# Clustered attention before two expert layers: products with the centroids at once in four column tiles, beside a block of products with v

## The chip, the cores and the metric

One core of a Trainium2 chip runs the kernel in one launch. The metric is device time in microseconds (us), over three runs of the kernel before: median 624.69, from 623.21 to 628.34. In the profile the engines are PE (TensorE matmuls), PEld (its weight loads), DVE (VectorE), ACT (ScalarE), POOL (GpSimd) and SP (the queue from which nearly all DMAs are issued).

## The reference

Attention in which a token only sees the tokens of its own cluster, then two layers of routed experts. Two batches, 8 heads, 768 tokens, head size 64, 16 centroids per head, all in 32-bit floats:

```python
q_n, k_n, c_n = (x / (norm(x) + 1e-6) for x in (q, k, centroids))
q_assign = argmax(einsum('bhsd,hcd->bhsc', q_n, c_n))
k_assign = argmax(einsum('bhsd,hcd->bhsc', k_n, c_n))
mask = q_assign[:, :, :, None] == k_assign[:, :, None, :]
scores = where(mask, q @ k.T / sqrt(64), -1e9)
attn = softmax(scores)
x = attn @ v                      # then (1536, 512)
x = moe(x, w_gate, w1, w2, capacity)      # top 1 of 8 experts, 512 -> 1024 -> 512, at most `capacity` tokens each
x = moe2(x, w_gate, w_output_gate, w1, w2)  # top 1 of 8, no capacity
```

## The kernel before

The attention is worked off in 8 **pairs**: a pair is one batch and two neighbouring heads j = 0, 1. A pair has 12 **slots**: one for each block c of 128 queries (c = 0 to 5) and each head j. One pass of the main loop (`for i in range(len(seq) + LAG + 1)`) is a slot. The program is not rescheduled: each engine works through its instructions in the order in which the Python code issues them. In a slot stand, in this order:

- `scores` (pss, L238): four matmuls into one of two PSUM tiles; its tile is free when the exp of the slot two before has read it. Then `softmax_max` (nm, L246) on DVE.
- `tr_p` (ppt, L268): the transposes of the exp of two slots before, in two halves of three, each half into one of the three PSUM tiles of the pool `ps_t`; each half is copied out to pt (L270), the first by ACT, the second by DVE, but by ACT too where c is 2 or 5.
- in slots 0, 4, 6 and 10 `av` (L280), a block of products with v; in slots 1 and 7 `fin`, with px (L307) on PE and its evictions on DVE.
- the loads of a later pair (slots 7, 8, 9: q, k, v), and the **preparation of the next pair**, one entry of the list `prep` per slot.
- `softmax_exp` (pe, L254) on ACT, behind what the preparation gave to ACT.

The preparation splits q and k into a rounded part and a rest (qh and kh on ACT, ql on DVE, kl on POOL), copies them by DMA into the operands of the scores (12 DMAs, `operands`), and finds each token's cluster: `logits` (plog, L153: products of the 32 padded centroids of two heads with q and with k, 384 tokens at a time), evicted to lt with a scale (L156 on ACT for the first half of the tokens, L160 on DVE for the second), `logits_t` (plt, L167: six transposes), `argmax` and `first` (DVE and POOL), and `oh_t` (poh, L194: six transposes of the one-hot rows, evicted by DVE to ot, L195), from where four DMAs bring the one-hot rows into the operands x2 and y2. The scores of the next pair wait for those.

All these transposes, plog and px take their PSUM tiles from the same three of `ps_t`; the one that was read longest ago is taken next. The DMAs of SP use eight completion semaphores in turn, and a DMA waits until the one eight before it on SP has landed. In pair 6 SP also issues the first four loads of expert weights (raw, 1 MB each, L808 and L810). In its slot 9 the pools of the preparation are closed, and the first converted weights (wh, L837, on ACT) take over their memory, so wh waits for the DMAs that read ot.

The slots of the preparation before: 0 qh; 1 ql, kh, kl; 2 logits; 3 logits_t; 4 argmax and operands; 5 first; 8 oh_t. In pair 0 it starts two slots later. The next pair is prepared in pairs 0 to 6. The first pair is prepared ahead of the loop.

Of the kernel before, what the change touches and what calls it, by code (L numbers as in the profile page):

```python
# [8 lines left out]
F32 = mybir.dt.float32  # L9
F32R = mybir.dt.float32r  # L10
I32 = mybir.dt.int32
AF = mybir.ActivationFunctionType
ALU = mybir.AluOpType
AX = mybir.AxisListType
PSUM = bass.MemoryType.PSUM
BIG = float(2.0 ** 100)
WARM = 8
P0 = 2
# [10 lines left out]
def attention(tc, end, ps_t, ident, wu, q, k, v, centroids, wg, x_half, lg_sb, consts, before_half, after_half, extra, slot):  # L29


    nc = tc.nc
    B, NP, P, _, C, D = v.shape
    H = 2 * NP
    S = P * C
    G = centroids.shape[1] // H
    E = wg.shape[1]
    HALF = C // 2
# [4 lines left out]
    with ExitStack() as ctx:  # L43
# [11 lines left out]
        def cpy(dst, src):  # L55
            nc.sync.dma_start(dst.bitcast(F32), src.bitcast(F32))

        def centroid_norms():

            nc.vector.tensor_tensor(c_sq, cw, cw, op=ALU.mult)  # L60
            p = ps_t.tile([P, 512], F32, tag="t", name="pc")[:64, :NP]
            for hp in range(NP):
                for t in range(2):
                    nc.tensor.matmul(p[32 * t:32 * t + 2 * G, hp:hp + 1], c_sq[:, hp].rearrange("p j g -> p (j g)"),
                                     ones, start=True, stop=True)
            nc.scalar.sqrt(c_n, p)
            nc.vector.tensor_scalar_add(c_n, c_n, 1e-6)
            nc.vector.reciprocal(c_n, c_n)
# [23 lines left out]
        c_sq = one.tile([P, NP, 2, G], F32, name="c_sq")  # L92
        c_n = one.tile([64, NP], F32, name="c_n")
        ones = one.tile([P, 1], F32, name="a_ones")
        rev = one.tile([P, G], F32, name="rev")
        msc = one.tile([64, 2], F32, name="msc")
        rw = end.tile([P, NP, P + 2 * E], F32, name="rw")
# [47 lines left out]

        def logits(pi):
            b, hp = pairs[pi]
            d = st[pi]
            d["lt"] = lt = w1.tile([64, S], F32, tag="lt", name="lt")
            for hf in range(2):  # L150
                p = ps_t.tile([P, 512], F32, tag="t", name="plog")[:64, :W]
                for t, nm in enumerate("qk"):
                    nc.tensor.matmul(p[32 * t:32 * t + 2 * G], cw[:, hp].rearrange("p j g -> p (j g)"),  # L153
                                     d[nm][:, hf * W:(hf + 1) * W], start=True, stop=True)
                if hf == 0:
                    nc.scalar.mul(lt[:, :W], p, c_n[:, hp:hp + 1])  # L156
                elif pi == 0:
                    nc.scalar.mul(lt[:, W:], p, c_n[:, hp:hp + 1])
                else:
                    nc.vector.tensor_scalar_mul(lt[:, W:], p, c_n[:, hp:hp + 1])  # L160

        def logits_t(pi):
            d = st[pi]
            p = ps_t.tile([P, 512], F32, tag="t", name="plt")[:, :C * 4 * G]
            d["lg"] = p.rearrange("p (c t j g) -> p c t j g", c=C, t=2, j=2)
            for c in range(C):
                nc.tensor.transpose(p[:, c * 4 * G:(c + 1) * 4 * G], d["lt"][:, c * P:(c + 1) * P], ident[:64, :64])  # L167

# [18 lines left out]
        def oh_t(pi):  # L187
            d = st[pi]
            ot = w1.tile([64, S], F32R, tag="lt", name="ot")
            ohv = d["oh"].rearrange("p (c i) g -> p c (i g)", i=4)  # L190
            for hf in range(2):
                p = ps_t.tile([P, 512], F32, tag="t", name="poh")[:64, :W]
                for c in range(HALF):
                    nc.tensor.transpose(p[:, c * P:(c + 1) * P], ohv[:, hf * HALF + c], ident)  # L194
                nc.vector.tensor_scalar(ot[:, hf * W:(hf + 1) * W], p, msc[:, 0:1], msc[:, 1:2],  # L195
                                        op0=ALU.mult, op1=ALU.add)
            s = pi % 2
            for j in range(2):
                cpy(xs["x2", s, j][64:64 + G], ot[j * G:(j + 1) * G])
                cpy(xs["y2", s, j][64:64 + G], ot[(2 + j) * G:(3 + j) * G])  # L200

# [17 lines left out]
        def first_rows(j):  # L219
            for hf in range(2):  # L220
                p = ps_t.tile([P, 512], F32, tag="t", name="poh")[:64, :W]
                for c in range(HALF):
                    nc.tensor.transpose(p[:, c * P:(c + 1) * P],
                                        oh0[j][:, hf * HALF + c].rearrange("p t g -> p (t g)"), ident)
                hs = slice(hf * W, (hf + 1) * W)
# [120 lines left out]
        def last():  # L346
# [3 lines left out]
        prep = [  # L350
            lambda i: part(i, "qh"),
            lambda i: (part(i, "ql"), part(i, "kh"), part(i, "kl")),
            lambda i: logits(i),
            lambda i: logits_t(i),
            lambda i: (argmax(i), operands(i, 0), operands(i, 1)),
            lambda i: first(i),
            lambda i: None,
# [19 lines left out]
        for j in range(2):  # L377
            nc.gpsimd.memset(oh0[j], 0.0)
        for (p0, c0, x) in ((0, 0, 1.0), (0, 1, 0.0), (32, 0, BIG), (32, 1, -BIG)):
            nc.vector.memset(msc[p0:p0 + 32, c0:c0 + 1], x)  # L380
        keep_warm(WARM)
# [48 lines left out]
        for i in range(len(seq) + LAG + 1):  # L430
# [15 lines left out]
            if cur:  # L446
# [7 lines left out]
                if i == 1:  # L454
                    first_rows(1)
                ps = sl - P0 + (sl - P0 > 6) if pi == 0 else sl
                if pi + 1 < NPR and 0 <= ps < len(prep):
# [1470 lines left out]
```

## Time and profile before

| | us |
|---|---|
| median of three runs | 624.69 |
| the profiled execution, its own time | 626.9 |
| its span | 625.1 |
| PE busy | 568.9 (91%) |
| DVE busy | 467.7 (75%) |
| ACT busy | 420.6 (67%) |
| POOL busy | 214.3 (34%) |
| start of slot 0 of pairs 1 to 7 | 41.50, 72.20, 103.23, 135.00, 168.60, 200.52, 234.33 |

The attention lasts until about 276 us; behind it the two expert layers follow, with 349 us. A time in a timeline is counted from the start of the span. A busy time of PE counts overlapping matmuls once; a product of 32-bit floats appears as two instructions, so the products of one half of the tokens (q and k) are four rows.

### The profile page before, as it was taken

Reading aid. Unit: us, or ns where it says so; the run is one execution under the profiler, and the core shown is the slowest. Engines: PE = TensorE matmul, PEld = TensorE weight load, DVE = VectorE, ACT = ScalarE, POOL = GpSimd, SP = SyncE. Lnnn points to the kernel's source line nnn. Section 1 sums busy time; section 2 is a strip of 40 time slices with the busy share of each in tenths; the row PEclk is TensorE's granted clock in tenths of the full one; section 3 lists DMA queues with packets and bytes.
Section 4 is the critical chain, followed back from the end, with each engine's and each line's share of the span. In section 5 each row is a group of like instructions: output and inputs, shape, how many; then the busy total and the mean of one; then the engine's idle time right before and its main releaser. Section 6 shows DMA issues by size and latency. Waiting matters only on the chain.

```text
span 625.1 us, 14529 instructions
## 1 busy us (share of the span) xinstructions
PE 568.9 (91%) x5430; PEld 469.5 (75%) x5430; DVE 467.7 (75%) x1214; ACT 420.6 (67%) x891; POOL 214.3 (34%) x425
## 2 busy tenths in 40 slices
PE   6899999998999988976999998998887899999993
PEld 2666767675766666655878997997766888999992
DVE  5867777679989677866597689788876566889881
ACT  4766666776666669843676776876853466979781
POOL 8702020204150210135725257444333523253441
PEclk9899999999999999999899999999989799999997
DMA  5879381926429961323386776977844457998930
GB/s 144 214 227 274 102 212 48 212 62 151 141 84 229 248 183 70 134 105 108 116 268 209 241 251 174 301 246 236 280 158 165 147 178 238 302 304 297 328 116 20
DMA packets 75518, 117.55 MB, mean 188 GB/s; under 512 B 10504, under 2 KB 43400, under 8 KB 75441
## 3 DMA queue, kind: packets, MB, share of 16 engines
q1 hardware_dynamic: 72017, 106.76, 56.6%
q0 software_dynamic: 3264, 9.72, 4.9%
q8 instruction: 45, 0.74, 0.5%
q14 instruction: 32, 0.26, 0.1%
q10 hardware_dynamic: 160, 0.07, 0.0%
HBM read 84.28 MB, written 12.87 MB: 155 GB/s over the span
## 4 chain that ended last, share of the span: by engine, by line
PE 61%; DVE 16%; ACT 10%; DMA 5%; issue 4%; POOL 2%; SPq 0%; ACTq 0%; POOLq 0%; DVEq 0%
PE ph L947 16%; PE py L1019 11%; PE av L280 9%; PE pss L238 7%; PE ppt L268 6%; DVE nm L246 3%; DVE wl L844 3%; PE pz L994 3%; ACT pe L254 2%; PE pyo L1635 2%; PE pxt L924 2%; ACT wh L837 2%; ACT pt L270 1%; DMA xg<-x2d,idx 1%; DMA out<-xo,tk 1%
## 5 line engine op out<-in xcount | busy, mean ns | idle before, releaser
L844 DVE SCALAR_TENSOR_TENSOR wl<-raw,sw,wh 128x1024 f16<-128x1024 f32 x128 | 163.5, 1283 | 17.9 <-ACT wh L837 17.1
L837 ACT ACTIVATE wh<-raw,sw 128x1024 f16<-128x1024 f32 x128 | 145.8, 1146 | 3.1 <-DMA x<-ot 2.5
L246 DVE TENSOR_REDUCE nm<-pss 128x1 f32<-128x768 f32 x96 | 91.4, 952 | 41.1 <-PE pss L238 37.4
L947 PEld LDWEIGHTS <-wh 128*128 128x128 f16 x1152 | 90.4, 101 | 18.2 <-issue 13.4
L254 ACT ACTIVATE pe<-pss,nm 128x768 f32<-128x768 f32 x96 | 87.1, 907 | 24.2 <-DVE nm L246 24.2
L238 PE MATMUL pss<-y,x 128*128 128x384 f32 x384 | 93.6, 365 | 4.7 <-ACT pe L254 3.2
L268 PE MATMUL ppt<-ident,pe 128*128 128x128 f32 x576 | 80.3, 275 | 3.3 <-ACT pe L254 1.3
L238 PEld LDWEIGHTS pss<-y,x 128*128 128x128 f32 x384 | 63.2, 190 | 25.1 <-issue 13.0
L947 PE MATMUL ph<-xh,wh 128*128 128x192 f16 (+14 forms) x576 | 69.1, 244 | 9.8 <-DVE hl L956 6.7
L270 ACT COPY pt<-ppt 128x384 f32<-128x384 f32 x128 | 57.9, 482 | 29.2 <-PE ppt L268 28.8
L1019 PEld LDWEIGHTS <-wh 128*128 128x128 f16 x960 | 72.4, 99 | 4.6 <-issue 1.3
L268 PEld LDWEIGHTS ppt<-ident,pe 128*128 128x128 f32 x576 | 69.2, 142 | 8.9 <-ACT pt L270 2.3
L947 PE MATMUL ph<-xl,wh 128*128 128x192 f16 (+14 forms) x576 | 68.9, 244 | 0.2
L947 PE MATMUL ph<-xh,wl 128*128 128x192 f16 (+14 forms) x576 | 68.9, 244 | 0.0
L280 PE MATMUL av<-pt,v 128*64 128x384 f32 x384 | 68.8, 494 | 0.0
L949 ACT ACTIVATE hh<-ph 128x128 f16<-128x128 f32 (+14 forms) x144 | 44.0, 312 | 34.3 <-PE ph L947 31.5
L956 DVE SCALAR_TENSOR_TENSOR hl<-ph,hh 128x192 f16<-128x192 f32 (+14 forms) x138 | 44.4, 334 | 26.7 <-ACT hh L949 26.1
L1019 PE MATMUL py<-hh,wh 128*128 128x192 f16 (+13 forms) x480 | 46.7, 239 | 1.9 <-ACT hh L949 1.1
L947 PEld LDWEIGHTS <-wl 128*128 128x128 f16 x576 | 46.7, 101 | 2.1
L1019 PE MATMUL py<-hl,wh 128*128 128x192 f16 (+13 forms) x480 | 46.6, 239 | 0.8 <-DVE hl L956 0.6
L1019 PE MATMUL py<-hh,wl 128*128 128x192 f16 (+13 forms) x480 | 46.1, 239 | 0.0
L280 PEld LDWEIGHTS av<-pt,v 128*64 128x64 f32 x384 | 24.8, 136 | 28.4 <-issue 28.2
(322 smaller groups left out, 864.1 us busy)
## 6 DMA issues: line engine op xcount, KB each, us to landing
raw<-in_moe_w SPq DMA_DIRECT2D x64, 1024.0 KB
y<-kh SPq DMA_DIRECT2D x31, 192.0 KB
x<-qh SPq DMA_DIRECT2D x30, 192.0 KB
q<-in_q SPq DMA_DIRECT2D x8, 384.0 KB
k<-in_k SPq DMA_DIRECT2D x8, 384.0 KB
x<-ql SPq DMA_DIRECT2D x16, 192.0 KB
v<-in_v SPq DMA_DIRECT2D x8, 384.0 KB
out<-zt SPq DMA_DIRECT2D x1, 3072.0 KB
```

The lines of the kernel that those rows point to most:

```text
L238: nc.tensor.matmul(p[:, hf, :W], xx[:, c * P:(c + 1) * P], yy[:, hf * W:(hf + 1) * W], start=a, stop=o)
L246: nc.vector.tensor_reduce(nm, p[:, :, :W], axis=AX.XY, op=ALU.max, negate=True)
L254: nc.scalar.activation(pe, p[:, :, :W], AF.Exp, bias=d["nm", c, j], scale=1.0, accum_out=d["sm"][:, c, j:j + 1])
L268: nc.tensor.transpose(p[:, kc * P:(kc + 1) * P], pe[:, kh, kc * P:(kc + 1) * P], ident)
L270: eng(pt[:, kh * HALF:(kh + 1) * HALF, (c % HALF) * P:(c % HALF + 1) * P], p.rearrange("p (a b) -> p a b", a=HALF))
L280: nc.tensor.matmul(p[j * D:(j + 1) * D, :W], d["v"][:, j, kc, :], d["pt", hf, j][:, kc, :], start=(kc == 0), stop=(kc == C - 1))
L837: nc.scalar.activation(hi[:, :, s], x[:, :, s], AF.Copy, scale=sw)
L844: nc.vector.scalar_tensor_tensor(lo[:, :, s], x[:, :, s], sw, hi[:, :, s], op0=ALU.mult, op1=ALU.subtract, accum_out=fl)
L947: nc.tensor.matmul(p[:, :N], w[:, c, fs], x[:, c, :N], start=(k == 0), stop=(k == 11))
L949: nc.scalar.activation(hh[:, f, :N], p[:, :N], AF.Relu)
L956: nc.vector.scalar_tensor_tensor(hl[:, f, :N], p[:, :N], 0.0, hh[:, f, :N], op0=ALU.max, op1=ALU.subtract)
L1019: nc.tensor.matmul(p[:, :N], w[:, f, s], x[:, f, :N], start=(k == 0), stop=(k == 23))
```

## The change

- `logits` writes the products of both halves of the tokens into one PSUM tile: q and k of the first half into partitions 0 and 32, of the second into 64 and 96. One eviction over 128 partitions follows, on DVE (on ACT ahead of the loop), where there were two over 64 partitions, on ACT and DVE.
- `logits_t` and `oh_t` transpose 128 by 128 blocks, three each instead of six, and ot is evicted by one DVE instruction instead of two. The chunks of tokens stand in another order, which the indices follow.
- ot then holds each row in two halves, so eight DMAs of 16 x 384 bring it into x2 and y2, where there were four of 16 x 768.
- The preparation stands in other slots: 0 logits, behind the block of av; 1 logits_t and qh; 2 argmax, kh, kl; 3 ql; 4 first and operands; 7 oh_t. The list has eight entries instead of nine, so the pools of the preparation close in slot 8 of pair 6.
- In the start, the norms of the centroids are made for 128 partitions, and eight constants are set by POOL where DVE set four.

```diff
         def logits(pi):
-            d["lt"] = lt = w1.tile([64, S], F32, tag="lt", name="lt")
+            d["lt"] = lt = w1.tile([P, W], F32, tag="lt", name="lt")
+            p = ps_t.tile([P, 512], F32, tag="t", name="plog")[:, :W]
             for hf in range(2):
-                p = ps_t.tile([P, 512], F32, tag="t", name="plog")[:64, :W]
                 for t, nm in enumerate("qk"):
-                    nc.tensor.matmul(p[32 * t:32 * t + 2 * G], cw[:, hp].rearrange("p j g -> p (j g)"),
+                    r = 64 * hf + 32 * t
+                    nc.tensor.matmul(p[r:r + 2 * G], cw[:, hp].rearrange("p j g -> p (j g)"),
                                      d[nm][:, hf * W:(hf + 1) * W], start=True, stop=True)
-                if hf == 0:
-                    nc.scalar.mul(lt[:, :W], p, c_n[:, hp:hp + 1])
-                elif pi == 0:
-                    nc.scalar.mul(lt[:, W:], p, c_n[:, hp:hp + 1])
-                else:
-                    nc.vector.tensor_scalar_mul(lt[:, W:], p, c_n[:, hp:hp + 1])
+            if pi == 0:
+                nc.scalar.mul(lt, p, c_n[:, hp:hp + 1])
+            else:
+                nc.vector.tensor_scalar_mul(lt, p, c_n[:, hp:hp + 1])
...
-            for c in range(C):
-                nc.tensor.transpose(p[:, c * 4 * G:(c + 1) * 4 * G], d["lt"][:, c * P:(c + 1) * P], ident[:64, :64])
+            for c in range(HALF):
+                nc.tensor.transpose(p[:, c * P:(c + 1) * P], d["lt"][:, c * P:(c + 1) * P], ident)
...
         def oh_t(pi):
-            ot = w1.tile([64, S], F32R, tag="lt", name="ot")
-            ohv = d["oh"].rearrange("p (c i) g -> p c (i g)", i=4)
-            for hf in range(2):
-                p = ps_t.tile([P, 512], F32, tag="t", name="poh")[:64, :W]
-                for c in range(HALF):
-                    nc.tensor.transpose(p[:, c * P:(c + 1) * P], ohv[:, hf * HALF + c], ident)
-                nc.vector.tensor_scalar(ot[:, hf * W:(hf + 1) * W], p, msc[:, 0:1], msc[:, 1:2],
-                                        op0=ALU.mult, op1=ALU.add)
+            ot = w1.tile([P, W], F32R, tag="lt", name="ot")
+            ohv = d["oh"].rearrange("p (c i) g -> p c (i g)", i=8)
+            p = ps_t.tile([P, 512], F32, tag="t", name="poh")[:, :W]
+            for c in range(HALF):
+                nc.tensor.transpose(p[:, c * P:(c + 1) * P], ohv[:, c], ident)
+            nc.vector.tensor_scalar(ot, p, msc[:, 0:1], msc[:, 1:2], op0=ALU.mult, op1=ALU.add)
             for j in range(2):
-                cpy(xs["x2", s, j][64:64 + G], ot[j * G:(j + 1) * G])
-                cpy(xs["y2", s, j][64:64 + G], ot[(2 + j) * G:(3 + j) * G])
+                for t, nm in enumerate(("x2", "y2")):
+                    for hf in range(2):
+                        r = 64 * hf + (2 * t + j) * G
+                        cpy(xs[nm, s, j][64:64 + G, hf * W:(hf + 1) * W], ot[r:r + G])
...
         prep = [
-            lambda i: part(i, "qh"),
-            lambda i: (part(i, "ql"), part(i, "kh"), part(i, "kl")),
             lambda i: logits(i),
-            lambda i: logits_t(i),
-            lambda i: (argmax(i), operands(i, 0), operands(i, 1)),
-            lambda i: first(i),
+            lambda i: (logits_t(i), part(i, "qh")),
+            lambda i: (argmax(i), part(i, "kh"), part(i, "kl")),
+            lambda i: part(i, "ql"),
+            lambda i: (first(i), operands(i, 0), operands(i, 1)),
             lambda i: None,
             lambda i: None,
             lambda i: oh_t(i),
...
-                ps = sl - P0 + (sl - P0 > 6) if pi == 0 else sl
+                ps = sl - P0 if pi == 0 else sl
```

The order on PE in slots 2 and 3 of pair 1 before (pss scores, ppt transposes of the exp, plog the products with the centroids, plt their transposes):

```order
L268 MATMUL ppt<-ident,pe 128x128 x6
L153 MATMUL plog<-q,cw 32x384
L153 MATMUL plog<-k,cw 32x384
L153 MATMUL plog<-q,cw 32x384
L153 MATMUL plog<-k,cw 32x384
L238 MATMUL pss<-y_542,x_541 128x384 x2
L238 MATMUL pss<-y_11_172,x_11_171 128x384 x2
L268 MATMUL ppt<-ident,pe 128x128 x6
L167 MATMUL plt<-ident,lt 128x64 x6
```

The same on PE with the change, in slots 0 and 1 of pair 1 (av the products with v, px the normalisation):

```order
L281 MATMUL av_652<-pt_423,v 64x384
L281 MATMUL av_652<-pt_503,v 64x384
L155 MATMUL plog<-q,cw 32x384
L155 MATMUL plog<-k,cw 32x384
L155 MATMUL plog<-q,cw 32x384
L155 MATMUL plog<-k,cw 32x384
L239 MATMUL pss<-y_548,x_547 128x384 x2
L239 MATMUL pss<-y_11_172,x_11_171 128x384 x2
L269 MATMUL ppt<-ident,pe 128x128 x6
L308 MATMUL px<-rw,avo 128x144 x3
L168 MATMUL plt<-ident,lt 128x128 x3
```

The four products now follow the av block of slot 0, two slots earlier, and the three transposes of lt follow px in slot 1.

The order on ACT in slots 0 to 2 of pair 2 before (avo the eviction of av, pe the exp, pt the copies of ppt):

```order
L287 COPY avo<-av_1024 128x384
L122 ACTIVATE qh<-q 128x768
L254 ACTIVATE pe,sm<-pss,nm 128x768
L270 COPY pt_992<-ppt 128x3x128 x2
L126 CAST kh<-k 128x768
L254 ACTIVATE pe,sm<-pss,nm 128x768
L270 COPY pt_1127<-ppt 128x3x128
L156 ACTIVATE lt<-plog,c_n 64x384
L254 ACTIVATE pe,sm<-pss,nm 128x768
```

And with the change:

```order
L288 COPY avo<-av_1019 128x384
L255 ACTIVATE pe,sm<-pss,nm 128x768
L271 COPY pt_987<-ppt 128x3x128 x2
L122 ACTIVATE qh<-q 128x768
L255 ACTIVATE pe,sm<-pss,nm 128x768
L271 COPY pt_1127<-ppt 128x3x128
L126 CAST kh<-k 128x768
L255 ACTIVATE pe,sm<-pss,nm 128x768
```

qh and kh each come one slot later, and the eviction of lt is gone from ACT.

The order on SP in pair 4 before (x1d is a write of attention rows, q, k and v the loads of a later pair):

```order
L1492 DMA x1d<-x 128x1572
L114 DMA q<-in_q 128x768
L114 DMA k<-in_k 128x768
L56 DMA x_10_169<-ot 16x768
L56 DMA y_10_170<-ot 16x768
L56 DMA x_11_171<-ot 16x768
L56 DMA y_11_172<-ot 16x768
L111 DMA v<-in_v 128x768
```

And with the change:

```order
L1493 DMA x1d<-x 128x1572
L114 DMA q<-in_q 128x768
L56 DMA x_10_169<-ot 16x384 x2
L56 DMA y_10_170<-ot 16x384 x2
L56 DMA x_11_171<-ot 16x384 x2
L56 DMA y_11_172<-ot 16x384 x2
L114 DMA k<-in_k 128x768
L111 DMA v<-in_v 128x768
```

Eight DMAs of ot stand where there were four, and the load of k now stands behind them.

## Rows read from the trace of the kernel before

**Rows 1.** The page: busy time, share of the span and instructions of each engine.

```profile
PE 568.9 (91%) x5430; PEld 469.5 (75%) x5430; DVE 467.7 (75%) x1214; ACT 420.6 (67%) x891; POOL 214.3 (34%) x425
```

**Rows 2.** Windows, pairs 1 and 5: stretch; length, busy PE PEld DVE ACT POOL, clock, DMA.

```profile
41.50:72.20 30.70, 30.35 (x203) 21.98 (x202) 22.03 (x40) 20.48 (x45) 3.60 (x6) 1.00 0.77 219
...
168.60:200.50 31.90, 31.21 (x211) 22.15 (x210) 28.71 (x73) 21.08 (x47) 8.30 (x9) 1.00 0.52 133
```

**Rows 3.** PE's timeline in pair 1: start, us, what, idle before.

```profile
43.03 2.16 PE L280 MATMUL av<-pt,v 128*64 128x384 f32 x12
...
48.20 0.82 PE L268 MATMUL ppt<-ident,pe 128*128 128x128 f32 x6
48.95 0.51 PE L153 MATMUL plog<-q,cw 128*32 128x384 f32 x1
...
50.91 0.97 PE L238 MATMUL pss<-y,x 128*128 128x384 f32 x4
...
52.47 0.58 PE L167 MATMUL plt<-ident,lt 64*128 64x64 f32 x6
52.98 0.97 PE L238 MATMUL pss<-y,x 128*128 128x384 f32 x4
...
63.08 0.90 PE L307 MATMUL px<-rw,avo 128*128 128x144 f32 x6
63.72 0.96 PE L238 MATMUL pss<-y,x 128*128 128x384 f32 x4
...
65.17 0.92 PE L194 MATMUL poh<-ident,oh 128*64 128x128 f32 x6
65.85 0.94 PE L238 MATMUL pss<-y,x 128*128 128x384 f32 x4
```

**Rows 4.** PE's timeline in the expert layers: products in four tiles, and what follows.

```profile
344.67 0.72 PE L1663 MATMUL pq<-yt,wgc 128*32 128x304 f32 x8
345.32 0.38 PE L1036 MATMUL pq<-flt,ones 128*128 128x1 f32 x2
```

**Rows 5.** ACT's timeline, slots 0 to 2 of pair 1.

```profile
45.61 0.85 ACT L122 ACTIVATE qh<-q 128x768 fp32r<-128x768 f32 x1
46.36 0.89 ACT L254 ACTIVATE pe<-pss,nm 128x768 f32<-128x768 f32 x1
...
47.23 0.86 ACT L270 COPY pt<-ppt 128x384 f32<-128x384 f32 x2
47.97 0.86 ACT L126 CAST kh<-k 128x768 fp32r<-128x768 f32 x1
48.70 0.93 ACT L254 ACTIVATE pe<-pss,nm 128x768 f32<-128x768 f32 x1
```

**Rows 6.** DVE groups: line, what, count, busy us, mean ns, idle before.

```profile
L270 DVE COPY pt<-ppt 128x384 f32<-128x384 f32 x64 | 34.9, 546 | 0.1
...
L195 DVE TENSOR_SCALAR ot<-poh,msc 64x384 fp32r<-64x384 f32 x14 | 8.7, 660 | 0.0
...
L160 DVE TENSOR_SCALAR lt<-plog,c_n 64x384 f32<-64x384 f32 x7 | 4.2, 606 | 3.6 <-PE plog L153 3.6
```

**Rows 7.** Timelines of SP and ACT around the first weights, pair 6.

```profile
210.21 0.55 SPq L56 DMA_DIRECT2D x<-ql  x1
...
218.03 2.02 SPq L810 DMA_DIRECT2D raw<-in_moe_w  x2
...
229.41 0.59 SPq L56 DMA_DIRECT2D y<-ot  x1
...
231.87 1.15 ACT L837 ACTIVATE wh<-raw,sw 128x1024 f16<-128x1024 f32 x1 [2.46 <-DMA x<-ot]
```

**Rows 8.** Window at the end of pair 6, columns as in rows 2.

```profile
226.00:230.00 4.00, 4.00 (x31) 3.23 (x30) 4.00 (x7) 2.39 (x5) 1.11 (x1) 1.00 0.57 165
```

**Rows 9.** One DMA of ot on SP, and the scores that waited for it on PE.

```profile
196.87 0.54 SPq L56 DMA_DIRECT2D y<-ot  x1
...
202.00 0.59 PE L238 MATMUL pss<-y,x 128*128 128x384 f32 x2 [0.89 <-DMA y<-ot]
```

More of the change, by code (lines that the diff above doesn't have):

```diff
@@ L60, in centroid_norms @@
             nc.vector.tensor_tensor(c_sq, cw, cw, op=ALU.mult)
-            p = ps_t.tile([P, 512], F32, tag="t", name="pc")[:64, :NP]
+            p = ps_t.tile([P, 512], F32, tag="t", name="pc")[:, :NP]
             for hp in range(NP):
-                for t in range(2):
+                for t in range(4):
                     nc.tensor.matmul(p[32 * t:32 * t + 2 * G, hp:hp + 1], c_sq[:, hp].rearrange("p j g -> p (j g)"),
@@ L92, in attention @@
         c_sq = one.tile([P, NP, 2, G], F32, name="c_sq")
-        c_n = one.tile([64, NP], F32, name="c_n")
+        c_n = one.tile([P, NP], F32, name="c_n")
         ones = one.tile([P, 1], F32, name="a_ones")
         rev = one.tile([P, G], F32, name="rev")
-        msc = one.tile([64, 2], F32, name="msc")
+        msc = one.tile([P, 2], F32, name="msc")
         rw = end.tile([P, NP, P + 2 * E], F32, name="rw")
@@ L223, in first_rows @@
                     nc.tensor.transpose(p[:, c * P:(c + 1) * P],
-                                        oh0[j][:, hf * HALF + c].rearrange("p t g -> p (t g)"), ident)
+                                        oh0[j][:, 2 * c + hf].rearrange("p t g -> p (t g)"), ident)
                 hs = slice(hf * W, (hf + 1) * W)
@@ L378, in attention @@
             nc.gpsimd.memset(oh0[j], 0.0)
-        for (p0, c0, x) in ((0, 0, 1.0), (0, 1, 0.0), (32, 0, BIG), (32, 1, -BIG)):
-            nc.vector.memset(msc[p0:p0 + 32, c0:c0 + 1], x)
+        for p0 in (0, 64):
+            for (p1, c0, x) in ((0, 0, 1.0), (0, 1, 0.0), (32, 0, BIG), (32, 1, -BIG)):
+                nc.gpsimd.memset(msc[p0 + p1:p0 + p1 + 32, c0:c0 + 1], x)
         keep_warm(WARM)
```

## The prediction

> **What bounds the kernel now.** I read the busy shares first: PE is busy for 91% of the span [rows 1]. Then the windows by pair, since the change lies in the pairs only. In pair 1 PE is busy for 30.35 of 30.70 us and DVE for 22.03: PE bounds a quiet pair. Pair 5 carries routing work on DVE too, which is busy there for 28.71 of 31.90 us beside 31.21 of PE [rows 2]: in pairs 4 and 5 (both alike) DVE ends some stretches, and PE work that goes there comes back as waiting. Then PE's timeline of a quiet pair, for the cost of each step [rows 3]: what counts is the time from a step's start to the start of the next step, since matmuls overlap. Last the end of pair 6, where ACT stands for 2.46 us until the DMAs that read ot have landed, so that the first weights can take their memory [rows 7]; that stall is set by SP and the DMAs, not by PE.
>
> The sum is made against the profiled execution, 626.9 us, which lies 2.2 above the median of the three runs, 624.69; I carry the difference over to the median. About 1% (6.2 us) is what a measurement of this kernel can tell from no change.
>
> **The change part by part**, for one quiet pair.
>
> *Products with the centroids.* Before they take PE from 48.95 to 50.91, 1.96 us, with a wait for a PSUM tile between the two halves [rows 3]. Afterwards the four products stand in four column tiles of one PSUM tile. The kernel has four-tile products already: with 304 columns they hold PE from 344.67 to 345.32, 0.65 us [rows 4]; for 384 columns I scale that to 0.82. Gain 1.96 - 0.82 = 1.14. Bounds: nothing gained but the wait, if the tiles go two by two; or 1.3, if 0.65 holds for 384 columns too.
>
> *Transposes.* The six of lt take 52.47 to 52.98, 0.51; the six of the one-hot rows 65.17 to 65.85, 0.68. Three of 128 by 128 are half of a ppt group, (48.95 - 48.20)/2 = 0.38 [rows 3]. Gain 0.13 + 0.30 = 0.43.
>
> *Evictions.* ACT loses the one of lt, DVE one of two of ot, 0.66. The remaining ones have 128 partitions instead of 64: a copy of 128x384 takes 0.546 and the eviction of 64x384 0.606 [rows 6], so partitions do not set the time. In a quiet pair both engines have room, and this counts as nothing.
>
> *qh and kh one slot later on ACT.* This is what I expect to take part of the gain back. With logits gone from slot 2, slots 2 and 3 hold only scores and transposes on PE, 65.17 - 63.72 = 1.45 each at most. The scores of slot 4 need the exp of slot 2. From the copies of slot 1 ACT has to do: two copies 0.74, qh 0.75, exp 0.87, one copy 0.37, kh 0.73, exp 0.93 [rows 5], together 4.39, and it starts when half of the ppt group of slot 1 is done, some 0.5 after that group's start: done at 4.9. PE needs from the same start ppt 0.75, px 0.64, three transposes 0.38 and two slots of 1.45, 4.67. So PE waits 0.2 at least. The upper end is that all of kh falls on the path, 0.73. I take 0.4, between the two, as each hand-over adds something.
>
> *ql, argmax, first moved on DVE.* The same work in slots 1 to 5 as before. In slots 1 to 3 it is now denser, but slot 4 has an av block of 2.16 [rows 3] that covers a late maximum. Nothing; if that cover fails it is the third rival. The eq and kl of POOL move with it; POOL is busy for 3.60 us of pair 1 [rows 2] and covers them.
>
> *SP.* Four more DMAs of ot per pair, and k's load behind all eight. They are issued from slot 7, one earlier than before. The pitch is about 0.62, as the last four rows of their kind show (229.41 is the fourth; the first stood three pitches before) [rows 7]. So k is issued 5.0 us after ot is ready. In the new pair slot 7 starts at about 19.2 (20.1 before, plus 0.82 and 0.38 in slots 0 and 1, less 1.96 and 0.51, plus 0.4), ot is ready at 22.6, k issued at 27.6, of about 29.5. The products want it 3.6 us into the next pair (scores and transposes 1.45, av 2.16). That leaves 5.5 us for its landing. DMAs of ot took 229.41 to 231.87 = 2.5 us to land in one place [rows 7] and 196.87 to 202.00 = 5.1 in another, behind the loads of q and k [rows 9]. I cost it at nothing: both are under 5.5.
>
> So a quiet pair gains 1.14 + 0.43 - 0.4 = 1.17, bounds 0.8 and 1.57. Pairs 0 to 3 are counted so: 4.7. In pairs 4 and 5 I count only what DVE loses, 0.66 each: 1.3. Together 6.0 up to the start of pair 6.
>
> *The first weights.* Pair 6 starts at T = 200.5, and wh at 231.87 = T + 31.4. The two last weight loads are issued by 220.05 [rows 7], and the DMAs fall quiet inside the window from 226 to 230, share 0.57: at about 226 + 0.57 x 4 = 228.3 = T + 27.8 [rows 8]. With the change x<-ql, which all operands behind it on SP queue for, waits for ql in slot 3 instead of slot 1: slot 3 starts at about T + 8.3, and scores, maximum, a copy and ql follow, so T + 11.9 where it was 210.21 = T + 9.7. The weight loads stand behind the operands and land 2.2 later, at T + 30.0, unless the transfers make up the gap. Of the eight DMAs of ot the seventh and eighth reuse the semaphores of these two loads, eight places before them on SP; before, the four of ot did not reach that far. They leave at T + 30.0 and 30.6 and land 2.5 later: wh at T + 33.1. If the transfers catch up fully, T + 30.9. I take T + 32.4, nearer to the later end because SP hands out work in order: 1.0 to 1.1 later than before, relative to the pair. ACT's wait is passed on to PE in full, as before. Pair 7 prepares nothing and the expert layers are unchanged; I pass what is left on to the end.
>
> *Start.* POOL and PE get a few short instructions more, DVE four fewer. I count nothing, 0.3 either way.
>
> **Sum**: 4.7 + 1.3 - 1.1 = 4.9. 626.9 - 4.9 = 622.0 for a profiled execution; 624.69 - 4.9 = **619.8** for the median.
>
> **The rivals.**
>
> *Nothing is given back.* PE gains 1.57 in all seven pairs, 11.0, and wh moves with the pair: 613.7. For it: PE is the busiest engine everywhere, ACT and DVE have 8 us of room in pair 1 [rows 2]. Against it: the room does not lie in slots 1 and 2. Chance 0.20.
>
> *k comes late, slower.* From a landing of 5.5 us on, the products at the head of a pair stand and PE with them; the scores of slot 1 are queued behind. Were it 8.0 each time, 2.5 per pair against 1.17 gained: 7 x 1.3 = 9.3, with the 1.1 of wh 10.4 slower, 635.1. It decides at 5.5; 5.1 is on record with two loads ahead [rows 9], now only q's is. Chance 0.07.
>
> *DVE ends slots 1 to 3.* From the end of the products it has lt 0.6, three maxima, px's evictions, two copies, argmax and ql, some 7.2 us by the pitches of such instructions (0.87, 1.1, 0.5, 1.1, 0.87), while PE is back at slot 4's maximum after 2.5 + 2.9 + 0.9 = 6.3. Uncovered, the 0.9 eats the rest of a quiet pair's gain but 0.3: 4 x 0.3 + 1.3 - 1.1 = 1.4, 623.3. Against it: the av block of slot 4. The Trainium skill, TensorEngine Tiling (Array Packing), Performance Considerations (PSUM Bottleneck), speaks for this rival: tiling speeds up TensorE but not the emptying of PSUM, which may become the bottleneck, and both ScalarE and VectorE should do it; here one of them is dropped. The traces bear it out only so far that DVE is the nearer of the two. Chance 0.14.
>
> *Not four at once.* If the tiles with different moving data run two by two, the products take 1.5 and not 0.82: 7 x 0.7 = 4.8 less, 624.6. Against it: the 0.65 for 304 columns, also with four different operands [rows 4]. Chance 0.06.
>
> **How the numbers follow.** My forecast has 0.53. Its own range is 616 to 623: the bounds of a quiet pair give 1.5 either way, wh 1.6, both rarely together. A quarter of it lies below 618.4. Faster by over 1%: 0.20 + 0.13 = 0.33. Slower by over 1% (from 631): most of the second rival, 0.06. Within 1%: the rest, 0.61. The range from 613.5 to 625.5 takes in the first, third and fourth case; left out are the second and the ends.
>
> **What would show it.** Per pair: four plog rows that start within 0.05 us of each other, and the next scores about 0.8 later; about 29.5 us from pair to pair in pairs 1 and 2; a PE wait of 0.2 to 0.7 in front of the scores of slot 4, released by pe; wh waiting for DMA of ot longer than 2.46. It would be wrong if plog waits for a DMA of k, if PE waits in slot 4 are over 1 us, or if wh starts less than 31 us into pair 6.

## The result

The changed kernel takes 633.65 us (median of four runs, 632.95 to 634.82) where the kernel before takes 624.55 (four runs, 623.21 to 628.34). The ratio of the runs on record is 1.0101, interval 1.0055 to 1.0148; the two medians alone would give 1.0146. A second set of runs on another chip gives 1.0116 (1.0063 to 1.0169). The forecast was 619.8, faster by 0.8%; the change is slower: by 1.0 to 1.2% in the two ratios, by 9.1 us between these medians.

The profiled execution took 633.55 (span 631.8). Its stretches stand against those of the first profile of before like this, from the starts of slot 0:

| stretch | before | after | difference | forecast |
|---|---|---|---|---|
| up to pair 0 | 12.81 | 12.17 | -0.6 | 0 |
| pair 0 | 28.69 | 29.03 | +0.3 | -1.2 |
| pair 1 | 30.70 | 37.94 | **+7.2** | -1.2 |
| pairs 2 and 3 | 62.80 | 60.93 | -1.9 | -2.3 |
| pairs 4 and 5 | 65.52 | 64.68 | -0.8 | -1.3 |
| pair 6 | 33.81 | 38.21 | **+4.4** | +1.1 with pair 7 |
| pair 7 to its last scores | 30.74 | 32.50 | +1.8 | |
| the rest | 360.0 | 356.3 | -3.7 | 0 |

The rest is no gain of the change: in the first profile of before the expert layers had a stretch at a granted clock of 0.83 (290 to 310 us). From the last maximum of the attention to the end the two profiles of before take 357.8 and 355.4, the two of after 354.1 and 356.6.

### The profile page after: what moved, and what is told of

Read it like the earlier page. It is cut to its first block, busy times and chain, and to the rows that moved or that the text cites. A ratio compares the mean times of both kernels' runs of the same rounds, so it can differ in the third digit from the quotient of the medians.

```text
span 631.8 us, 14473 instructions
## 1 busy us (share of the span) xinstructions
PE 562.5 (89%) x5400; PEld 465.3 (74%) x5401; DVE 468.3 (74%) x1203; ACT 415.5 (66%) x883; POOL 211.3 (33%) x433
## 4 chain that ended last, share of the span: by engine, by line
PE 58%; DVE 17%; ACT 9%; DMA 8%; issue 4%; POOL 1%; SPq 0%; ACTq 0%; DVEq 0%; POOLq 0%
PE ph L948 14%; PE py L1020 13%; PE av L281 9%; PE pss L239 8%; PE ppt L269 6%; DVE nm L247 3%; DVE wl L845 3%; ACT pe L255 3%; DMA xg<-x2d,idx 2%; PE pyo L1636 2%; DMA raw<-in_moe_w 2%; PE pz L995 2%; PE pxt L925 2%; DVE ql L124 1%; ACT wh L838 1%
## 5 line engine op out<-in xcount | busy, mean ns | idle before, releaser
L269 PE MATMUL ppt<-ident,pe 128*128 128x128 f32 x576 | 82.5, 278 | 4.5 <-ACT pt L271 2.5
L281 PE MATMUL av<-pt,v 128*64 128x384 f32 x384 | 71.1, 508 | 0.0
```

The costliest lines, as they stand in the source:

```text
L269: nc.tensor.transpose(p[:, kc * P:(kc + 1) * P], pe[:, kh, kc * P:(kc + 1) * P], ident)
L281: nc.tensor.matmul(p[j * D:(j + 1) * D, :W], d["v"][:, j, kc, :], d["pt", hf, j][:, kc, :], start=(kc == 0), stop=(kc == C - 1))
```

## The profile after

PE is busy for a smaller share, with less work; DVE and ACT hardly change (compare [rows 1]):

```profile
PE 562.5 (89%) x5400; PEld 465.3 (74%) x5401; DVE 468.3 (74%) x1203; ACT 415.5 (66%) x883; POOL 211.3 (33%) x433
```

The windows by pair (columns as in [rows 2]), first of the kernel before, pairs 2 and 3, then of after, pairs 1, 2, 3 and 6:

```profile
72.20:103.23 31.03, 30.68 (x207) 22.28 (x205) 23.25 (x44) 20.86 (x46) 4.45 (x6) 1.00 0.56 137
103.23:135.00 31.77, 30.77 (x207) 22.32 (x206) 23.60 (x49) 23.70 (x58) 4.52 (x6) 1.00 0.55 133
```

```profile
41.20:79.14 37.94, 32.35 (x197) 22.68 (x196) 22.98 (x39) 19.90 (x44) 4.17 (x6) 0.91 0.66 190
79.14:109.72 30.58, 29.41 (x201) 21.73 (x199) 23.12 (x43) 20.37 (x45) 3.73 (x6) 1.00 0.56 137
109.72:140.07 30.35, 29.49 (x202) 21.77 (x200) 24.05 (x48) 23.08 (x57) 3.73 (x6) 1.00 0.54 135
...
204.75:242.96 38.21, 29.53 (x197) 21.51 (x196) 25.28 (x46) 21.20 (x46) 5.02 (x7) 0.96 0.70 202
```

In the quiet pairs 2 and 3 the change does about what it was counted for: PE is busy 1.27 and 1.28 us less, the pairs are 0.45 and 1.42 shorter, 1.87 together where 2.3 was forecast. In pairs 1 and 6 PE stands for 5.6 and 8.7 us (length less busy time). PE's timeline at the head of pair 1 (start, us, what, idle before) shows the first of the two places:

```profile
41.20 0.60 PE L239 MATMUL pss<-y,x 128*128 128x384 f32 x2
46.27 0.98 PE L239 MATMUL pss<-y,x 128*128 128x384 f32 x2 [4.48 <-DMA y<-ot]
47.05 1.48 PE L269 MATMUL ppt<-ident,pe 128*128 128x128 f32 x6
48.46 4.00 PE L281 MATMUL av<-pt,v 128*64 128x384 f32 x12
52.39 0.51 PE L155 MATMUL plog<-q,cw 128*32 128x384 f32 x1
...
52.75 0.49 PE L155 MATMUL plog<-k,cw 128*32 128x384 f32 x1
53.17 0.97 PE L239 MATMUL pss<-y,x 128*128 128x384 f32 x4
```

The eight rows of plog start within 0.36 us and the next scores 0.78 after the first of them: all four products do run at once (0.82 was forecast, 1.96 was it before). But the scores of slot 0 wait 4.48 us for one-hot rows, and behind the wait PE runs at half clock: ppt takes 1.48 where it took 0.82, av 4.00 where it took 2.16 [rows 3]. From 41.20 to 53.17 it is 11.97 us; the same stretch of pair 2 takes 4.40 (79.14 to 83.54). So 7.57 us are lost here, 4.48 in the wait and 3.09 to the clock. SP's queue shows why the rows were late:

```profile
30.19 0.46 SPq L56 DMA_DIRECT2D x<-ql  x1
...
37.37 0.89 SPq L114 DMA_DIRECT2D q<-in_q  x1
38.36 0.87 SPq L114 DMA_DIRECT2D k<-in_k  x1
39.28 0.42 SPq L111 DMA_DIRECT2D v<-in_v  x1
39.80 1.22 SPq L56 DMA_DIRECT2D x<-ot  x2
...
44.30 1.72 SPq L56 DMA_DIRECT2D y<-ot  x2
```

ot was ready at 37.6, but the DMAs of ot stand on SP behind three loads of 384 KB, these behind the operands, and these behind ql. The last two leave only at 44.30 to 46.02, and reuse the semaphores of the loads of k and v. But the wait does not hang on these two: the scores of slot 0 need only the first four, and by the landing times in the trace the fourth, issued at 41.69 without a wait, landed at 46.24, when PE starts. So the wait is the queue behind the loads. Before, x<-ql left at 25.19 and v at 34.91.

The second place is the first wh in pair 6. SP, then ACT, then PE:

```profile
218.85 0.46 SPq L56 DMA_DIRECT2D x<-ql  x1
...
226.11 2.02 SPq L811 DMA_DIRECT2D raw<-in_moe_w  x2
...
235.02 4.07 SPq L56 DMA_DIRECT2D y<-ot  x2
```

```profile
240.50 1.15 ACT L838 ACTIVATE wh<-raw,sw 128x1024 f16<-128x1024 f32 x1 [9.17 <-DMA y<-ot]
```

```profile
242.96 1.65 PE L239 MATMUL pss<-y,x 128*128 128x384 f32 x4 [7.64 <-ACT pe L255]
244.40 1.49 PE L269 MATMUL ppt<-ident,pe 128*128 128x128 f32 x6
245.82 2.61 PE L281 MATMUL av<-pt,v 128*64 128x384 f32 x12
248.36 0.97 PE L239 MATMUL pss<-y,x 128*128 128x384 f32 x4
```

wh waits 9.17 us and not 2.46 [rows 7]. The weight loads leave 21.4 us into the pair (17.5 before), and the DMAs of ot land behind them: by the landing times in the trace the second load at 238.56, the seventh DMA of ot at 239.97, and the eighth, which waited for that load's semaphore and was issued at 238.58, at 240.39. Here too the clock falls: from the transposes at 234.50 to the scores of slot 1 it is 13.86 us, before 6.19 (231.77 to 237.96), 5.90 of it more waiting and 1.77 the clock. The granted clock of the two stretches is the third number from the end of these rows:

```profile
46.27:53.17 6.90, 6.90 (x28) 3.17 (x29) 1.51 (x2) 1.14 (x3) 0.00 (x0) 0.57 0.68 232
...
242.96:248.36 5.40, 5.40 (x23) 3.40 (x23) 0.97 (x3) 3.21 (x6) 0.00 (x0) 0.65 0.00 0
```

Why x<-ql was so late stands in two timelines, DVE's and POOL's:

```profile
121.61 2.20 DVE L124 SCALAR_TENSOR_TENSOR ql<-q,qh 128x768 fp32r<-128x768 f32 x1
...
185.06 1.39 DVE L124 SCALAR_TENSOR_TENSOR ql<-q,qh 128x768 fp32r<-128x768 f32 x1
...
216.37 2.44 DVE L124 SCALAR_TENSOR_TENSOR ql<-q,qh 128x768 fp32r<-128x768 f32 x1
```

```profile
121.16 1.84 POOL L128 TENSOR_TENSOR kl<-k,kh 128x768 fp32r<-128x768 f32 x1
...
184.62 1.01 POOL L178 TENSOR_TENSOR eq<-eq,rev 128x384 f32<-128x384 f32 x1
185.59 2.54 POOL L128 TENSOR_TENSOR kl<-k,kh 128x768 fp32r<-128x768 f32 x1
...
216.18 1.83 POOL L128 TENSOR_TENSOR kl<-k,kh 128x768 fp32r<-128x768 f32 x1
```

ql takes 0.95 us by itself. Where it starts while POOL is at kl or eq, it ends 0.80 to 0.82 us after that instruction does: 123.81 after 123.00, 186.45 after 185.63, 218.81 after 218.01; the other four pairs give 0.82 each. And kl, begun while ql runs, takes 2.54 and not 1.83. They do not share, the later one waits for the whole of the earlier one; in the profile this is no wait but a long instruction.

## The experiments

The runs came to five chips, each beside runs of the kernel before on the same chip, whose times reach from 624.2 to 637.1. In some executions PE is slow at the very start (in e3_again at a granted clock of 0.50 from 8 to 12 us; a row of another stands below, with f4_before_rv) and pair 0 begins up to 3 us later; so beside each ratio stands the attention's own length, from the start of the first maximum (nm) on DVE to the start of the last, in the profiled execution.

| kernel | ratio to before (interval) | attention | wait, head of pair 1 | wait, first wh |
|---|---|---|---|---|
| before, two profiles | 1 | 252.4, 252.5 | 0 | 2.46, 2.46 |
| changed, two profiles | 1.0101 (1.0055 to 1.0148), 1.0116 (1.0063 to 1.0169) | 263.4, 261.5 | 4.48, 4.81 | 9.17, 9.16 |
| e1_four | 1.0168 (1.0123 to 1.0213) | 267.9 | 5.39 | 7.82 |
| e2_apart | 1.0040 (1.0007 to 1.0073) | 259.8 | 3.77 | 8.47 |
| e3_eight, two profiles | 0.9991 (0.9957 to 1.0024) | 258.3, 257.7 | 0 | 6.79, 5.66 |
| e4_places | 0.9938 (0.9907 to 0.9969) | 255.6 | 2.32 | 7.89 |
| e5_pe | 0.9919 (0.9893 to 0.9945) | 251.7 | 0.92 | 3.38 |
| f1_raw | 1.0015 (0.9979 to 1.0052) | 258.7 | 5.85 | 4.16 |
| f2_best | 0.9879 (0.9828 to 0.9930) | 247.9 | 0 | 2.38 |
| f3_apart_raw | 0.9890 (0.9853 to 0.9927) | 250.4 | 2.27 | 4.24 |
| f4_before_rv | 1.0018 (0.9990 to 1.0047) | 253.5 | 0 | 2.38 |
| h_kl | 1.0121 (1.0072 to 1.0170) | 264.0 | 4.97 | 9.37 |
| g_best2 | 0.9859 (0.9815 to 0.9904) | 247.8 | 0 | 2.67 |
| g_best3 | 0.9867 (0.9820 to 0.9913) | 245.7 | 0 | 4.42 |

Two theories stood at first: **A**, the eight DMAs of ot, and **B**, the late ql. The times expected of the first four were meant beside a kernel before of 624.55; the ratios are turned into such times below.

### e1_four: four DMAs of ot in the changed kernel

```diff
-            ot = w1.tile([P, W], F32R, tag="lt", name="ot")
+            ot = w1.tile([64, S], F32R, tag="lt", name="ot")
...
-                        cpy(xs[nm, s, j][64:64 + G, hf * W:(hf + 1) * W], ot[r:r + G])
+                cpy(xs["x2", s, j][64:64 + G], ot[j * G:(j + 1) * G])
+                cpy(xs["y2", s, j][64:64 + G], ot[(2 + j) * G:(3 + j) * G])
```

> The changed kernel, but ot is made as before the change: two halves of 64 partitions, six transposes, two evictions, four DMAs of 16x768. Everything else, the places of the preparation too, is as changed. Theory A (the loss of 9.1 us comes from the eight DMAs of ot: the last of them wait on SP for big loads that stand eight places before them, the wait of 4.48 us at the head of pair 1 and the 9.17 us in front of wh): both waits shrink to under 2.5 and under 5, the half clock behind them goes, time 619 to 625. Theory B (ql is late, since it runs beside kl and takes up to 2.44 us, and all operands, loads and DMAs of ot queue behind it; eight or four does not matter): both waits stay over half their size, time 629 to 633.

Slower still (635, outside both ranges of time), and both waits are there, 5.39 and 7.82, over half their size, as B had it. A falls as the whole cause. In pair 6 no DMA of ot waits for a semaphore now, and wh is late all the same; SP, then ACT:

```profile
232.46 1.48 SPq L811 DMA_DIRECT2D raw<-in_moe_w  x2
...
236.76 0.59 SPq L56 DMA_DIRECT2D y<-ot  x1
```

```profile
245.32 1.15 ACT L838 ACTIVATE wh<-raw,sw 128x1024 f16<-128x1024 f32 x1 [7.82 <-DMA x<-ot]
```

From the issue of the last DMA of ot (48 KB, 236.76) to the end of wh's wait it is 8.6 us, where it was 2.5 before [rows 7]; the 2 MB of weights left just ahead. Pairs 2 to 5 take 0.56 us each more than with three transposes (128.5 against 126.2 together, counted from maximum to maximum).

### e2_apart: ql and kl not at the same time

```diff
-            lambda i: (argmax(i), part(i, "kh"), part(i, "kl")),
-            lambda i: part(i, "ql"),
+            lambda i: (part(i, "ql"), argmax(i), part(i, "kh")),
+            lambda i: part(i, "kl"),
```

> The changed kernel, but ql stands one slot earlier, at the head of slot 2, and kl one slot later, in slot 3, so that DVE's ql and POOL's kl no longer run at the same time. Eight DMAs of ot stay. Both theories: ql takes 0.95 us as before the change. Theory A (eight DMAs of ot): the operands leave SP 2 to 3 us earlier, the waits for DMAs of ot at the head of pair 1 and in front of wh shrink by about that but stay over 1.5 and over 6, time 624 to 629. Theory B (late ql): both waits go, time 616 to 621.

ql takes 0.95 in all pairs:

```profile
24.79 0.95 DVE L124 SCALAR_TENSOR_TENSOR ql<-q,qh 128x768 fp32r<-128x768 f32 x1
```

The time falls from 1.0116 to 1.0040, 627, in A's range; the waits stay over 1.5 and over 6, as A had it, but do not shrink by its 2 to 3, and B's end of both waits did not come. The wait at the head of pair 1 shrinks by only 0.7 to 1.0, because PE, too, comes earlier there (39.8 and not 41.8): x<-ql leaves 2.9 us earlier (27.34), and the wait ends 2.7 earlier (43.61). wh is held as before.

### e3_eight: eight DMAs of ot in the kernel before

```diff
-                cpy(xs["x2", s, j][64:64 + G], ot[j * G:(j + 1) * G])
-                cpy(xs["y2", s, j][64:64 + G], ot[(2 + j) * G:(3 + j) * G])
+                for t, nm in enumerate(("x2", "y2")):
+                    for hf in range(2):
+                        hs = slice(hf * W, (hf + 1) * W)
+                        cpy(xs[nm, s, j][64:64 + G, hs], ot[(2 * t + j) * G:(2 * t + j + 1) * G, hs])
```

> The kernel before the change, with one edit: each of the four DMAs of ot is split into two of 16x384, in the same order. Theory A (eight DMAs reach back to loads on SP): a wait for a DMA of ot of 1 to 3 us at the head of pair 1, wh 1 to 2 us later than 31.4 us into pair 6, quiet pairs unchanged, time 626 to 631. Theory B (late ql): no wait worth 1 us, time 624 to 626.

No wait at the head of pair 1: there A is wrong. In front of wh it is 6.79. Ten times show no difference, though, so a second profile was taken:

> e3_eight unchanged, a second execution with a profile: the first showed a wait of 6.79 us in front of wh, and yet its ten times are not longer than those of the kernel before. Eight DMAs reach back to the weight loads (A): the wait in front of wh is 5 to 8 us again. Rival: the wait of the first profile came from that one execution, in which the start ran at half clock and pair 0 began 3 us later; with a start like that of the kernel before, the wait is 2.4 to 4.5.

ACT in the two profiles:

```profile
239.44 1.15 ACT L839 ACTIVATE wh<-raw,sw 128x1024 f16<-128x1024 f32 x1 [6.79 <-DMA y<-ot]
```

```profile
235.37 1.15 ACT L839 ACTIVATE wh<-raw,sw 128x1024 f16<-128x1024 f32 x1 [5.66 <-DMA y<-ot]
```

The last two DMAs of ot on SP, in the same two profiles:

```profile
233.97 4.05 SPq L56 DMA_DIRECT2D y<-ot  x2
```

```profile
231.03 2.92 SPq L56 DMA_DIRECT2D y<-ot  x2
```

So eight DMAs alone make wh wait 3.2 to 4.3 us longer: the last two, which reuse the semaphores of the two weight loads, take 4.05 and 2.92 us on SP, where two of before took 1.2. A holds at this place. That the timed ratio shows none of it stays open; the profiled executions (632.78 and 631.02) lie in the upper half of its times.

### e4_places and e5_pe: the places of before

The preparation goes back to its old slots; e4_places keeps the rest of the change, e5_pe has the four DMAs and six transposes of ot of before as well, so only logits and logits_t are new.

```diff
         prep = [
-            lambda i: logits(i),
-            lambda i: (logits_t(i), part(i, "qh")),
...
+            lambda i: part(i, "qh"),
+            lambda i: (part(i, "ql"), part(i, "kh"), part(i, "kl")),
+            lambda i: logits(i),
+            lambda i: logits_t(i),
+            lambda i: (argmax(i), operands(i, 0), operands(i, 1)),
...
```

> The changed kernel with the preparation back in the slots of the kernel before (qh; ql, kh, kl; logits; logits_t; argmax and operands; first; oh_t in slot 8). The products in four column tiles, the three transposes and the eight DMAs of ot stay. Theory A (eight DMAs): quiet pairs gain 1.2 to 1.6 us against before, the head of pair 1 and wh lose 3 to 6 together, time 619 to 624. Theory B (late ql): the full gain shows, time 614 to 618.

> Only the part of the change that works on PE in the first half of the preparation: the products in four column tiles and the three transposes of lt. The places in the slots and ot with its four DMAs are those of the kernel before. Theory C: quiet pairs take 1 to 1.6 us less; the wait at the head of pair 1 is 0.5 to 2 (PE arrives earlier, the transfers do not) and the one in front of wh 3 to 8, since the two weight loads still stand ahead of the DMAs of ot; 0.988 to 0.994 of the time before. Rival (eight DMAs cost time, A): both waits as before, 0.985 or less.

Now the kernel is faster than before, 0.9938 (620.7, in A's range) and 0.9919. In e4_places pairs 2 and 3 take 59.7 us, 1.55 each less than before (62.8) and 0.6 less than with the new places (60.9): there the new places give back 0.6 per pair. In pairs 4 and 5 it is the other way round, 65.5 us together with the old places and 64.7 with the new. The two waits of e4_places are 2.32 and 5.43 longer than before, more than A's 3 to 6. In e5_pe everything lies in C's ranges: 1.05 less per quiet pair, waits of 0.92 and 3.38. Theory **C** came out of the first four runs: the DMAs of ot queue behind megabytes that SP issued just ahead of them, and how late those are is decided by the operands, and so by ql. A second profile of the kernel before (b_again) was to show whether wh waits longer where the execution takes longer; it met a short one (624.56, wait 2.46 again), and so decides nothing.

### f1_raw: the weight loads behind the DMAs of ot, in the changed kernel

```diff
-         (-2, 4): ('load',),
-         (-2, 6): ('load',),
-         (-2, 9): ('open_ring', 'open_first', 'piece'),
-         (-2, 10): ('gather',),
+         (-2, 9): ('open_ring', 'open_first', 'piece', 'load'),
+         (-2, 10): ('gather', 'load'),
```

> The changed kernel with one edit: the last two weight loads of pair 6 (1 MB each) are issued in slots 9 and 10, behind the eight DMAs of ot, not in slots 4 and 6. Theory C: the wait of 9.17 us in front of wh falls under 1.5, the half clock behind it goes, 7 to 10 us less than the changed kernel, so 0.995 to 1.000 of the time before; the wait at the head of pair 1 stays at 4 to 5. Rival (the late operands hold the DMAs of ot themselves, the loads do not matter): the wait stays over 5, 1.004 to 1.010.

Pair 6 falls from 38.2 to 32.5 us (counted from maximum to maximum), the wait from 9.17 to 4.16:

```profile
236.62 1.15 ACT L838 ACTIVATE wh<-raw,sw 128x1024 f16<-128x1024 f32 x1 [4.16 <-DMA y<-ot]
```

That is C's direction and not all of its size: under 1.5 was expected, and 1.0015 lies between C and its rival. What is left is the eight issues themselves (229.27 to 235.03 on SP) and a landing.

### f2_best, f3_apart_raw and f4_before_rv: the loads moved in three kernels

In all three the load of v stands in slot 10, so that in pair 0 it follows the DMAs of ot, and the weight loads stand as in f1_raw. f2_best is e5_pe with that, f3_apart_raw is e2_apart with that, f4_before_rv is the kernel before with that.

```diff
-LD = {7: "q", 8: "k", 9: "v"}
+LD = {7: "q", 8: "k", 10: "v"}
```

> The kernel of e5_pe with the big loads behind the DMAs of ot at both places: in pair 0 the load of v in slot 10 and not 9, in pair 6 the last two weight loads in slots 9 and 10. Theory C: no wait over 1 us at the head of pair 1, nor in front of wh; quiet pairs 1 to 1.6 less; 0.975 to 0.985 of the time before. Rival: as e5_pe, since the first big loads of the later weights then come late, 0.988 to 0.994.

> The changed kernel, products at once, three transposes, eight DMAs of ot, with three moves: ql into slot 2 and kl into slot 3 (they no longer run side by side), the load of v into slot 10, behind the DMAs of ot of pair 0, and the last two weight loads of pair 6 into slots 9 and 10, behind the DMAs of ot. Theory C (late operands, then DMAs of ot queued behind big loads): the moves of ql and of the loads add up, head of pair 1 waits 2 to 3 us, wh under 4, 0.990 to 0.996 of the time before. Rival (the eight DMAs and the places of logits in slot 0 are the loss themselves): 0.998 or more.

> The kernel before, with only the loads moved: v into slot 10, the last two weight loads of pair 6 into slots 9 and 10, behind the DMAs of ot. Theory C: the kernel before has nearly no wait at the head of pair 1 and 2.46 us in front of wh, so the moves alone give 0 to 2.5 us, 0.996 to 1.000. Rival (the gain of f2_best, 1.2%, comes from these moves and not from the products): 0.988 to 0.993.

f2_best, at 0.9879, lies over C's range and at the lower end of its rival's: the wait at the head of pair 1 is gone, as C had it, the 2.38 in front of wh are not. f3_apart_raw (0.9890, just under the range expected; wh's 4.24 just over; 2.27 left at the head of pair 1, where q and k still stand ahead) keeps every product, transpose and DMA of the change and is 1.1% faster than before, where the change is 1.2% slower: the moves of ql and kl and of the loads together are worth 2.3%. f4_before_rv, with the loads moved alone, gains nothing (1.0018, interval from 0.9990): before, they stood in nobody's way (2.38 in front of wh, as with 2.46). So the gain of f2_best and f3_apart_raw is that of the products and transposes, once nothing takes it back. The slow start, in f4_before_rv; these rows took 0.49 in the two profiles of before. The granted clock is given as 1.00 in this stretch, so what slowed them stays open:

```profile
7.74 0.85 PE L153 MATMUL plog<-q,cw 128*32 128x384 f32 x1
```

### g_after and h_kl: the changed kernel again, and kl one slot later

> The changed kernel, unchanged, on the chip and beside the runs of the experiments. 1.007 to 1.013 of the time before; the waits at the head of pair 1 (4 to 6 us) and in front of wh (8 to 10) as in its first profile.

g_after repeats the waits within 0.4 us. In h_kl kl is issued in slot 4:

```diff
-            lambda i: (argmax(i), part(i, "kh"), part(i, "kl")),
+            lambda i: (argmax(i), part(i, "kh")),
             lambda i: part(i, "ql"),
-            lambda i: (first(i), operands(i, 0), operands(i, 1)),
+            lambda i: (part(i, "kl"), first(i), operands(i, 0), operands(i, 1)),
```

> The changed kernel with one edit: kl on POOL one slot later (slot 4), so that it no longer runs beside ql, which stays in slot 3. Theory D (the two exclude each other, and whichever starts second waits for the other to end): ql takes 0.95 us again in all pairs, the scores of pairs 0 to 6 that follow ql no longer wait (1.55 at 31.58 us), the operands leave 1.3 to 1.5 us earlier, and the waits at the head of pair 1 and for wh shrink by 0 to 1.5; 1.005 to 1.010 of the time before. Rival (ql is slow for another reason in slot 3, as the transfers into the tiles it reads or writes): ql stays over 1.3.

It told nothing of D, since it changed nothing; DVE, then POOL:

```profile
27.46 2.44 DVE L124 SCALAR_TENSOR_TENSOR ql<-q,qh 128x768 fp32r<-128x768 f32 x1
```

```profile
27.25 1.83 POOL L128 TENSOR_TENSOR kl<-k,kh 128x768 fp32r<-128x768 f32 x1
```

A slot is an order on each engine, not a time. POOL had nothing else between eq and kl, so kl still ran right behind eq, beside ql. What D rests on is the ends of the instructions in the profile after, and e2_apart.

### g_best2 and g_best3: the best order, with four and with eight DMAs

Both are f2_best with oh_t in slot 7 instead of 8 (one of the empty entries of prep is gone); g_best3 has the one-hot rows of the change.

> f2_best with the one-hot rows (oh_t) one slot earlier, in slot 7, in pairs 1 to 6. Theory C: the DMAs of ot of pair 6 leave 2 us earlier, so the 2.38 us in front of wh and the 1.36 at the head of pair 6 fall under 0.5; 0.982 to 0.987 of the time before. Rival (wh would wait for something else, its raw data or the eviction): as f2_best, 0.988.

> As g_best2, but with the one-hot rows as in the change: three transposes, one eviction, eight DMAs of ot of 16x384. It parts what eight DMAs cost from what they save on PE, once no big load stands ahead of them. Theory C: quiet pairs take 0.3 to 0.6 us less than in g_best2, the wait in front of wh grows by 1 to 2, since four more DMAs leave SP at 0.63 us each; 0.981 to 0.988 of the time before. Rival (eight DMAs cost on their own): 0.990 or more, with waits for DMAs of ot over 1 us at the heads of several pairs.

0.9859 and 0.9867, as expected: both beat the kernel before, by 1.3 to 1.4%, and the changed one, by 2.5%. The wait at the head of pair 6 (1.36 in f2_best) went, but wh still waits 2.67 in g_best2, as the rival had it in size, though not in its reason: it waits for a DMA of ot, one landing behind the last issue. The earlier oh_t has a price, too: pairs 2 and 3 take 61.7 us together, where they took 60.7 in f2_best. Eight DMAs and three transposes save 0.33 us in each of pairs 2 to 5 (126.8 against 128.1 together, from maximum to maximum) and cost 1.75 more in front of wh (4.42): about nothing in all.

## Why the prediction was wrong, point by point

- **Products and transposes**: right. plog 0.78 for 0.82 forecast; the transposes 0.24 and 0.25 (55.37 to 55.61, 70.68 to 70.93) for 0.38. With the old places a quiet pair gains 1.55, the 1.57 of the upper bound.
- **qh and kh later on ACT**: right in kind. In pair 1 the scores of slot 4 wait 0.39 for pe, behind kh, as forecast (0.4); in pair 2 ppt waits 0.69 in slot 3 for a copy by ACT, in pair 3 nothing waits in slot 4. The 0.6 that the new places cost in pairs 2 and 3 (e4_places) is for the most part something else, the next point; that it is near 0.4 is luck.
- **oh_t in slot 7**: a term that the sum lacked. From the scores of slot 7 to those of slot 10 it is 5.64 us in pairs 2 and 3, with oh_t in slot 8 (e4_places) 5.20, and 5.59 and 5.82 before: here the gain of the one-hot transposes is gone again. g_best2, whose only edit against f2_best is this one, shows it too (6.21 for 5.59 and 5.82). In slot 7 ot's eviction stands on DVE behind those of px, the maximum comes late, and with it pe and the scores; DVE, then PE, in pair 2:

```profile
101.62 0.55 DVE L324 TENSOR_TENSOR x<-px,ri 128x384 f32<-128x384 f32 x1
102.08 0.67 DVE L195 TENSOR_SCALAR ot<-poh,msc 128x384 fp32r<-128x384 f32 x1
102.67 0.94 DVE L247 TENSOR_REDUCE nm<-pss 128x1 f32<-128x768 f32 x1
```

```profile
104.69 0.97 PE L239 MATMUL pss<-y,x 128*128 128x384 f32 x4 [0.23 <-ACT pe L255]
```

- **"ql, argmax, first ... Nothing" and POOL that "covers" eq and kl**: wrong. I asked whether POOL had time, not what it does to DVE beside it. ql took 1.30 to 2.50 in pairs 0 to 6. In pairs 2 and 3 the av block did cover that, as said; in pair 1 the scores of slot 6 waited 0.49. But in pair 0, whose preparation starts two slots later, it held the next scores for 1.55 us and sent the operands off 5 us later than before (30.19 against 25.19), of which 1.5 are kl and the rest two slots.
- **"SP ... I cost it at nothing"**: the step that failed most. I followed k's load into the next pair, and plog never waited for it. What I did not follow was the queue in pair 0, where the loads stand *ahead* of the DMAs of ot and all of it behind ql. The DMAs of ot landed in time in the kernel before; how little slack they had no row of idle time shows. Price: 7.57 us, with the clock.
- **The first weights**: right in the last link, size off. wh was forecast at T + 32.4 and started at T + 35.7. x<-ql left at T + 14.1 and not T + 11.9, and the second weight load landed at T + 33.8 and not T + 30.0; the eighth DMA of ot, which waited for it, landed 1.8 later. That link alone is not the cause: the seventh landed only 0.4 before the eighth, and with four DMAs wh waits 7.82 (e1_four). A DMA of ot behind 2 MB takes about 8 us and not the 2.5 that I took from a place with nothing ahead.
- **The clock** had no term at all: 3.09 (part of the 7.57) and 1.77 us behind the two waits.
- **The rivals**: the slower one (635.1) came near in time, with another mechanism: a wait at two places, not one of k in seven pairs. That DVE holds PE up early in a pair happened in pairs 0 and 1, through ql and not through the eviction of lt. The rule of the Trainium skill, TensorEngine Tiling (Array Packing), Performance Considerations, that emptying PSUM may become the bottleneck, did not decide the result: DVE was as busy in pair 2 as before (23.12 and 23.25). Evictions do hold PE up in slots 7 to 9, but because of where oh_t stands.

The sum: 8.4 us missed in pair 1, 1.5 in pair 0, 5.1 in pairs 6 and 7, 1 in the rest; less the start (0.6) and the layers (3.7, above) that makes the 11.6 between -4.9 and +6.7 of the profiled executions.

## What to carry to other kernels

A step that is moved takes its DMAs with it, and these meet others: write down, for the tightest place in the program (the shortened first round, the last one), what stands on the queue ahead of each small DMA that somebody waits for, and when it last landed in time by luck. Put big loads behind small urgent ones; here that and parting two instructions turned 1.2% slower into 1.1% faster, with the same work. And before two elementwise steps on DVE and GpSimd fall into one slot, look whether both read two SBUF tensors.

## What the runs showed of the hardware

DVE's ql (two inputs in SBUF) and GpSimd's kl and eq exclude each other for whole instructions: in seven of seven pairs the end of ql lies 0.80 to 0.82 us behind that of the GpSimd instruction that was running when it began, and so it does in the profiles of g_after, h_kl, f1_raw and e1_four. Beside the kl of e2_apart, DVE's maximum (0.96) and its copy of pt (0.55), which read PSUM, take their usual time. The Trainium skill, SBUF — State Buffer, SBUF: two separate sides, says just that of a VectorE operation with two SBUF inputs beside a GpSimd operation that reads SBUF: the two share a pair of ports, an exclusive lock that whoever starts first holds for the whole instruction. The trace agrees; what it adds is that the profile shows this as busy time (2.44 for 0.95) and as no wait.

After 4.48 us with no work PE ran the next 6.9 us at a granted clock of 0.57, mostly the lower of its two levels (1.2 GHz), though busy without a gap; behind the wait of 7.64 it cost 1.77. Both long waits of this kernel cost more than themselves.
